# Four key blocks of an attention unit accumulate in one PSUM pair; one addition and the queries' sum go to accumulating DMAs

## The chip, the cores and the metric

One core of one Trainium2 chip runs the whole program. The metric is the device time of one execution in microseconds (us). Each kernel is given by the median of several executions and by one more execution that the hardware profiler recorded. The engines are named as in the profile: PE is TensorE's matmul side and PEld its weight loads, DVE is VectorE, ACT is ScalarE, POOL is GpSimd, and SP is SyncE, which here only issues DMAs. Every engine works through its own instructions in order and waits on semaphores of the others.

## The reference

Three stages follow one another; the change is in the first.

```python
# attention: q, k, v are (4, 8, 1152, 64) float32
q_pool = q.reshape(B, H, S // 2, 2, D).mean(axis=3)
scores = scale * np.matmul(q_pool, k.transpose(0, 1, 3, 2))
scores = scores - np.max(scores, axis=-1, keepdims=True)
attn = np.exp(scores)
attn = attn / (np.sum(attn, axis=-1, keepdims=True) + 1e-09)
x = np.matmul(attn, v)                 # 2304 tokens of 512 after a transpose
# then a dense layer: h = x @ w_in; g = h * np.cos(h); x = g @ w_out
# then a soft mixture of 8 experts with 4 slots each
```

## The kernel before

Attention handles two heads at a time, a *pair* p of 16; a pair has two halves of 288 pooled queries, and one half of a pair is a *unit* (32 units). Keys are cut into 9 *blocks* t of 128. For a unit the scores of one block are a [128 keys, 2 heads, 288 queries] tile in a PSUM pair (two banks); three such pairs (`BANKS = 3`) rotate, the fourth holds the output `o`.

- `operands` loads a pair: SP's DMAs bring `qr` (both members of each pooled pair of queries, 576 KB), `kr` (576 KB) and `vr`; DVE adds the two halves of `qr` into `qs` (`pooled`, L260); ACT makes bf16 copies `qb` and `kb` (L263).
- `maximum` finds a bound of the maximum for every query: 14 *rounds* a pair, each four bf16 matmuls into one PSUM pair (L305) and one DVE reduction of it (L310, tile `mp`). Two small transposes by PE (L317), reductions into `mc` (L324, L329) and ACT (L343) turn the result into the diagonal matrices `D`, which hold the negated maxima.
- `half_of` runs a unit. For each block, `products` (L409) multiplies keys by pooled queries in float32, `maxima` (L418) adds the negated maxima by four bf16 matmuls of ones with `D` into the same PSUM pair, ACT takes the exponential into a buffer `e` (L423, 8 buffers), and `av` (L431) accumulates `e` times values into `o`. The sums over keys are made beside it: DVE adds four of the blocks' `e` and POOL the other five (`ADD_BY`, L440), DVE joins the two (L443).
- `finish` takes the unit's output: ACT and DVE copy it out (L498, L502), PE sums over partitions (L511), small DMAs of SP spread the reciprocals (L526, L536, L540), POOL scales (L543) and makes low parts (L555).

The order is not the order of the text: `Plan` collects all operations with costs and due times, and fixes an order for every engine. The due times come from the spacing `P` of blocks and from the tables `ROUNDS` (when each round is due) and `DUES`. Two weight chunks of the next stage are decoded meanwhile (`FIRST`, lines from L707). From 389.6 us on, PE works on the dense layer (L780).

Of the kernel before, what the change touches and what calls it, by code (L numbers as in the profile page):

```python
# [10 lines left out]
FP32 = mybir.dt.float32  # L11
# [124 lines left out]
class Attention:  # L136
# [16 lines left out]
    FIRST_ROUNDS = (-13, -12, -11, -10, -9, -8, -7, -5, -7.2, -4.0, -2.3, -1.6, 0.9, 2.4)  # L153
    E_BUFS = 8

    BEHIND = 13.8

    DUES = {
        "load": 1.4, "free": 4.4, "v": 23.6, "pooled": 11.1, "qb": 3.0, "kb": -23.2, "top": -45.4,
        "diagonal": 50.2, "add": 31.2, "whole": -30.9, "take": -41.6, "join": -9.5, "sums": 14.9, "out": -15.9,  # L160
        "fold": -26.2, "inv": -14.5, "row": 30.0, "spread": 13.4, "scale": -2.4, "high": 65.4, "low": 18.3,
    }
    JOIN_BY, SCALE_BY, LOW_BY = "V", "G", "G"

# [64 lines left out]
    def operands(self, p, m):  # L229
# [11 lines left out]
        def tiles():  # L241
            self.qr[p] = self.two.tile([128, 2, NQ], FP32, tag="qr", name="qr")
            self.kr[p] = self.three.tile([128, S], FP32, tag="kr", name="kr")
            self.qs[p] = self.three.tile([128, NQ], FP32, tag="qs", name="qs")
# [20 lines left out]
        ring = lambda names, size: [(n, size, (n, p)) for n in names]  # L265
        new = ring(["kr", "qs"], 3) + ring(["qr", "qb", "kb"], 2)
        first = op(m, "SP", 0.0, tiles, new=new, early=early)
        self.q_after[p], self.k_after[p], self.s_after[p] = {}, {}, []
        late = 0.0
        for i, (a, n) in enumerate(q_parts):  # L270
            x = op(m + 0.5 * i, "SP", 0.6, lambda a=a, n=n: load_q(a, n), [first], uses=[("qr", p)],
                   more=4.2 if p else (2.4, 2.8, 3.3)[i], early=early)
            x = op(at_("pooled", 0.1 * i) if p else m, "V", 0.07 + n / 960, lambda a=a, n=n: pooled(a, n), [x], uses=[("qr", p), ("qs", p)], port=True)
            self.s_after[p].append(x)
            c = op(at_("qb", 0.1 * i) if p else m + 1.0 + i, "A", 0.07 + n / 1180, lambda a=a, n=n: copy(self.qb, self.qs, a, n), [x],
                   uses=[("qs", p), ("qb", p)])
            for y in range(0, NQ, QB):
                if a <= y < a + n:
                    self.q_after[p][y // QB] = [c]
        for i, (a, n) in enumerate(k_parts):  # L280
            x = op(m + (0.1, 0.2)[i], "SP" if p else "A", 0.6, lambda a=a, n=n: load_k(a, n), [first], uses=[("kr", p)],
                   more=5.6 if p else (2.5, 3.6)[i], early=early)
            self.s_after[p].append(x)
            for y in range(a, a + n, KC):
                self.k_after[p][y // KC] = [op(at_("kb", 0.1 * i) if p else m + 1.1 + i + y / 1e4, "A", 0.405, lambda y=y: copy(self.kb, self.kr, y, KC), [x],
                                               uses=[("kr", p), ("kb", p)])]
        self.v_after[p] = op(at_("v"), "SP", 0.6, load_v, [] if p else self.k_after[0][NC - 1], new=[("vr", 2, ("vr", p))],
                             more=4.2, early=early + late)


    def maximum(self, p):
# [55 lines left out]
        for c, rounds in enumerate(self.rounds):  # L347
            for n, (combos, x) in enumerate(rounds):
# [6 lines left out]
                       uses=users)  # L355
                new = [("mp", 2, ("mp", p))] if i == 0 else []
                d = op(t, "V", 0.868, lambda i=i, x=x: reduce(i, x), [r], new=new,
                       uses=[key] + ([] if new else [("mp", p)]))
                reds.append(d)
# [30 lines left out]
    def half_of(self, p, c):  # L390
# [11 lines left out]
        def products(t, st):  # L402
            st["ps"] = ps = self.bank(("s", u, t), "s")
            s = slice(N * c, N * c + N)
            for h in range(2):
                x = slice(64 * h, 64 * h + 64)
                for y in (0, 64):
                    w = self.kr[p][x, 128 * t + y:128 * t + y + 64]
                    nc.tensor.matmul(ps[y:y + 64, h, 0:N], w, self.qs[p][x, s], start=True, stop=False)  # L409
# [37 lines left out]
        for t in range(J):  # L447
# [17 lines left out]

            who = self.ADD_BY[t]
            if who == "P":
# [3 lines left out]
            if who not in where:  # L471
# [5 lines left out]
            before = sts[t0] if count == 1 else None  # L477
            x = op(s + due["add"] * P, who, (0.667, 1.37)[who == "G"],
                   lambda who=who, st=st, before=before, new=bool(new): add(who, st, before, new), [e, last], new=new,
                   uses=[ke] + ([("e", u, t0)] if new else [key]), port=True)  # L480
            where[who] = (count + 1, t, x)
# [98 lines left out]
    def run(self, ident, others=()):  # L580
        P, J = self.P, self.J
        pair = 2 * J * P
        self.q_after, self.k_after, self.s_after, self.v_after, self.D_after, self.reds = {}, {}, {}, {}, {}, {}
        plan = self.plan
        for p in range(self.NP):
# [933 lines left out]
```

## Time and profile before

| | us |
|---|---|
| median of 3 runs (869.24 to 871.09) | 870.83 |
| the profiled execution | 872.76 |
| its span, first to last instruction | 870.5 |
| PE busy in the span | 847.4 |
| DVE, ACT, POOL busy | 704.2, 527.7, 390.6 |

Attention fills the span from about 7.5 to 398 us, the dense layer follows, and the experts take the last 70 us. Matmuls overlap: a row's time in the profile runs to the modelled end of its last matmul, while the next row on PE starts earlier. What a piece of work costs PE is therefore read from the start of its row to the start of the next.

### The profile page before, as it was taken

To read this page: it belongs to the slowest core of one execution; us is meant where nothing else is said; L and a number is where in the kernel's file an instruction comes from. 1 tells how busy PE (TensorE), PEld (TensorE's weight loads), DVE (VectorE), ACT (ScalarE), POOL (GpSimd) and SP (SyncE) were. 2 spreads that over 40 slices of the span, in tenths; PEclk is the share of its full clock that TensorE was granted. 3 is DMA by queue.
4 is the path that set the end of the run, shared out by engine and by line. 5 is a ranking of instruction groups with operands and counts; after the bars stand their busy time and mean duration, and the time that the engine had idled before them with its cause. 6 is when DMAs were issued, how large, how long until landed. Compare 5 with 4: busy or idle time off the path is not lost.

```text
span 870.5 us, 24363 instructions
## 1 busy us (share of the span) xinstructions
PE 847.4 (97%) x9901; PEld 612.2 (70%) x9901; DVE 704.2 (81%) x1309; ACT 527.7 (61%) x1132; POOL 390.6 (45%) x381
## 2 busy tenths in 40 slices
PE   5999999999999999999999999999999999999996
PEld 3666566656666666667788888888888888877355
DVE  6999999899899888855989888888899889544423
ACT  3777777767777777774875555555555555454223
POOL 0566656766666666664554333344433333220100
PEclk9999999999999999999999999999999999999898
DMA  7033323333333233111121111110111110594897
GB/s 254 15 94 113 112 74 90 98 106 101 101 101 88 80 101 101 46 44 44 54 61 50 36 37 49 49 48 29 49 49 49 38 36 13 226 422 151 317 423 227
DMA packets 53969, 90.89 MB, mean 104 GB/s; under 512 B 21473, under 2 KB 33505, under 8 KB 49761
## 3 DMA queue, kind: packets, MB, share of 16 engines
q1 hardware_dynamic: 53568, 88.76, 31.3%
q8 instruction: 77, 1.26, 0.6%
q10 hardware_dynamic: 288, 0.59, 0.2%
q14 instruction: 36, 0.29, 0.1%
HBM read 78.71 MB, written 4.72 MB: 96 GB/s over the span
## 4 chain that ended last, share of the span: by engine, by line
PE 91%; DVE 4%; ACT 2%; issue 1%; POOL 1%; DMA 1%; SPq 0%; DVEq 0%; ACTq 0%
PE ops L780 21%; PE hps L780 21%; PE o L431 16%; PE s L409 15%; PE m L305 4%; PE s L418 4%; PE hq L1341 2%; PE so L1384 2%; PE sums L511 1%; DVE mp L310 1%; PE xtp L961 1%; PE fo L1413 1%; DMA qr<-in_q_dram 1%; PE lgp L975 1%; PE sps L1160 1%
## 5 line engine op out<-in xcount | busy, mean ns | idle before, releaser
L310 DVE TENSOR_REDUCE mp<-m 128x2 f32<-128x768 f32 x224 | 203.6, 952 | 29.8 <-PE m L305 29.4
L423 ACT ACTIVATE e<-s 128x576 f32<-128x576 f32 x288 | 176.3, 653 | 53.2 <-PE s L418 50.7
L780 PE MATMUL ops<-w,g 128*128 128x512 f32 x864 | 206.3, 391 | 2.0 <-POOL g L818 1.4
L780 PE MATMUL hps<-x,w 128*128 128x512 f32 (+1 forms) x960 | 204.5, 368 | 0.0
L780 PEld LDWEIGHTS hps<-x,w 128*128 128x128 f32 x960 | 168.0, 188 | 31.7 <-issue 1.5
L780 PEld LDWEIGHTS ops<-w,g 128*128 128x128 f32 x864 | 160.7, 188 | 36.9 <-POOL g L818 2.4
L409 PE MATMUL s<-qs,kr 64*64 64x288 f32 x2304 | 180.5, 403 | 3.2 <-DVE mp L310 3.1
L431 PE MATMUL o<-e,vr 64*64 64x288 f32 x2304 | 181.0, 406 | 0.0
L818 POOL TENSOR_TENSOR g<-r,g 128x512 fp32r<-128x512 f32 (+1 forms) x80 | 100.1, 1252 | 147.3 <-ACT g L815 121.3
L440 POOL TENSOR_TENSOR acc<-acc,e 128x576 f32<-128x576 f32 x96 | 136.6, 1423 | 3.2 <-ACT e L423 0.9
L805 ACT ACTIVATE r<-r 128x512 f32<-128x512 f32 (+1 forms) x160 | 94.0, 587 | 69.4 <-DVE r L798 67.7
L440 POOL TENSOR_TENSOR acc<-e 128x576 f32<-128x576 f32 x32 | 48.5, 1517 | 153.5 <-ACT e L423 153.5
L409 PEld LDWEIGHTS s<-qs,kr 64*64 64x64 f32 x2304 | 79.7, 133 | 44.0 <-DVE mp L310 7.4
L431 PEld LDWEIGHTS o<-e,vr 64*64 64x64 f32 x2304 | 82.7, 133 | 31.8 <-issue 7.1
L741 POOL TENSOR_TENSOR da<-da,w 128x256 f32<-128x256 f32 x64 | 49.3, 771 | 94.6 <-DVE db L730 42.1
L418 PE MATMUL s<-D,a_ones 64*64 64x288 bf16 x1152 | 87.2, 283 | 0.0
L305 PE MATMUL m<-kb,qb 64*64 64x384 bf16 x896 | 74.0, 331 | 9.3 <-ACT qb L263 7.5
L798 DVE SCALAR_TENSOR_TENSOR r<-ki,hps 128x512 f32<-128x512 int32 (+1 forms) x80 | 50.4, 631 | 36.1 <-ACT ki L795 34.1
L815 ACT CAST g<-r 128x512 fp32r<-128x512 f32 (+1 forms) x80 | 46.2, 578 | 40.0 <-DVE r L808 37.5
L795 ACT ACTIVATE ki<-hps 128x512 int32<-128x512 f32 (+1 forms) x80 | 44.0, 551 | 39.1 <-PE hps L780 38.0
L941 DVE TENSOR_TENSOR acc<-acc,ops 128x512 f32<-128x512 f32 x70 | 47.7, 685 | 22.4 <-PE ops L780 22.4
L343 ACT ACTIVATE D<-a_minus,mc 128x64 bf16<-128x64 f32 x142 | 37.4, 336 | 33.1 <-DVE mc L324 32.9
(148 smaller groups left out, 952.5 us busy)
## 6 DMA issues: line engine op xcount, KB each, us to landing
raw<-in_w_io_dram SPq DMA_DIRECT2D x64, 256.0 KB
w1t<-in_w_dram SPq DMA_DIRECT2D x15, 1024.0 KB
vr<-in_v_dram SPq DMA_DIRECT2D x16, 576.0 KB
qr<-in_q_dram SPq DMA_DIRECT2D x15, 576.0 KB
kr<-in_k_dram SPq DMA_DIRECT2D x15, 576.0 KB
w2t<-in_w2b_dram SPq DMA_DIRECT2D x8, 1024.0 KB
r<-row SPq DMA_DIRECT2D x32, 144.0 KB
late<-in_w2a_dram SPq DMA_DIRECT2D x4, 1024.0 KB
```

The source lines that it names most:

```text
L305: nc.tensor.matmul(ps[heads[c], h.start // 64, 0:self.KC], w, m, start=True, stop=True)
L310: nc.vector.tensor_reduce(out=self.mp[p][:, x], in_=st[i][:, :, 0:self.KC], axis=AX.X, op=ALU.max)
L409: nc.tensor.matmul(ps[y:y + 64, h, 0:N], w, self.qs[p][x, s], start=True, stop=False)
L418: nc.tensor.matmul(ps[y:y + 64, h, 0:N], self.ones16[x], D[x, s], start=False, stop=True)
L423: nc.scalar.activation(out=st["e"], in_=st["ps"][:, :, 0:N], func=ACTF.Exp, scale=1.0 / 16.0)
L431: nc.tensor.matmul(self.o[u][64 * h:64 * h + 64, r, 0:N], self.vr[p][x, h, t], st["e"][x, h], start=(t == 0), stop=(t == J - 1),)
L440: self.engine(who).tensor_tensor(out=acc[who], in0=x, in1=st["e"], op=ALU.add)
L741: nc.gpsimd.tensor_tensor(out=st["a"], in0=st["a"], in1=fl(half(0)), op=ALU.subtract)
L780: nc.tensor.matmul(ps, x, y, start=(i == 0 and m == 0), stop=(i == n - 1 and m == 2))
L798: nc.vector.scalar_tensor_tensor(out=st["r"], in0=st["ki"], scalar=-c, in1=x, op0=ALU.mult, op1=ALU.add)
L805: nc.scalar.activation(out=st["r"], in_=st["r"], **kw)
L818: nc.gpsimd.tensor_tensor(out=g["l"][:, i], in0=st["r"], in1=fl(g["h"][:, i]), op=ALU.subtract)
```

## The change

In every pair but the first, the blocks of a unit that stand at four places (`CHAIN`: 0, 2, 5 and 7) share one PSUM pair. POOL replaces key block b by the difference of blocks b and b + 1 for three blocks of the pair (`delta`). The first of the four gets its scores and the maxima as before; each of the other three (`link`) adds a product with a difference of keys to what stands in PSUM, so that it needs no maxima, but must wait until ACT has read the scores before it. `block(t)` permutes the blocks so that the chain's keys lie together.

The sum over `e` of one block (lower case `v` in `ADD_BY`) is made by an accumulating DMA that POOL issues, and POOL adds one block less itself, so that DVE has as many additions as before. In all pairs but the first, SP loads one half of the queries straight into `qs`, and POOL issues a DMA that accumulates the other half; DVE's addition L260 goes away there. There are 10 buffers `e` instead of 8, one `qr`, and three `mp`. The tables of due times change.

```diff
-    P = 1.28
+    P = 1.267
-    ADD_BY = "VVVGGGGVG"
+    ADD_BY = "VVvVGGGGV"
-    ROUNDS = (-10.7, -8.2, -10.4, -9.8, -3.7, -4.8, -3.3, -0.8, -8.1, 0.5, 1.6, 2.2, 7.5, 7.7)
-    E_BUFS = 8
+    ROUNDS = (-12.3, -6.4, -10.3, -16.0, -5.0, -13.7, -8.0, -1.5, -2.5, 1.0, 1.3, 5.4, 0.2, 7.5)
+    E_BUFS = 10
+    ISSUE, LANDING = 0.95, 5.5
-    BEHIND = 13.8
+    BEHIND = 10.08
...
+    CHAIN, DELTA_BY = (0, 2, 5, 7), "G"
...
         def load_q(a, n):
-            nc.sync.dma_start(out=self.qr[p][:, :, a:a + n], in_=q[:, :, a:a + n])
+            if p:
+                nc.sync.dma_start(out=self.qs[p][:, a:a + n], in_=q[:, 0, a:a + n])
+            else:
+                nc.sync.dma_start(out=self.qr[p][:, :, a:a + n], in_=q[:, :, a:a + n])
...
         def pooled(a, n):
+            if p:
+                nc.gpsimd.dma_start(out=self.qs[p][:, a:a + n], in_=q[:, 1, a:a + n], accum_op=ALU.add)
+                return
...
+        if p:
+            n = 128 * (len(self.CHAIN) - 1)
+
+            def delta():
+                x = self.kr[p]
+                self.engine(self.DELTA_BY).tensor_tensor(out=x[:, 0:n], in0=x[:, 0:n], in1=x[:, 128:128 + n], op=ALU.subtract)
...
+        def link(t, st):
+            st["ps"] = ps = sts[links[0]]["ps"]
+            s, b = slice(N * c, N * c + N), 128 * block(t)
+            for h in range(2):
+                x = slice(64 * h, 64 * h + 64)
+                for y in (0, 64):
+                    w = self.kr[p][x, b + y:b + y + 64]
+                    out = ps[y:y + 64, h, 0:N]
+                    nc.tensor.matmul(out, w, self.qs[p][x, s], start=False, stop=True, skip_group_check=True)
...
-        def add(who, st, before, new):
+        def add(who, st, before, new, by_dma=False):
...
+            if by_dma:
+                nc.gpsimd.dma_start(out=acc[who], in_=st["e"], accum_op=ALU.add)
+                return
...
+            elif t in links[1:]:
+                ks = ("s", u, links[0])
+                x = es[links[links.index(t) - 1]]
+                a = op(s, "P", 0.486, lambda t=t, st=st: link(t, st), [x, *self.delta_after[p]], uses=[ks, *uses[:2]], name="scores")
...
-FIRST_FROM, FIRST_EVERY, FIRST_DUE = 2.14, -0.96, 1000
+FIRST_FROM, FIRST_EVERY, FIRST_DUE = 2.82, -0.24, 1000
```

Three places show what this does to the order. In the rows below, a name in brackets after *waits* is the semaphore of an engine or of a DMA queue: Activation is ACT's, Pool POOL's, DMASW that of DMAs issued by POOL, DMAHW that of DMAs issued by SP or ACT. Line numbers of the changed kernel are its own: L445 products, L454 maxima, L432 links, L329 rounds, L332 their reductions, L479 additions, L477 the accumulating DMA of a block, L268 that of the queries, L306 the differences of keys.

PE in the middle of a unit, before: each block's products are followed by the maxima's weights and matmuls (four pairs of such rows a block).

```order
L418 LDWEIGHTS a_ones_130
L418 MATMUL s<-D,a_ones_130 64x288
L409 MATMUL s<-qs,kr 64x288 x4
L418 LDWEIGHTS a_ones_130
L418 MATMUL s<-D,a_ones_130 64x288
```

PE in the middle of a unit, after: a link stands between two other blocks' work, and nothing but a wait for ACT comes with it.

```order
L454 MATMUL s<-D,a_ones_130 64x288
L432 MATMUL s<-qs,kr 64x288 [waits Activation_49]
L432 MATMUL s<-qs,kr 64x288 x3
L329 LDWEIGHTS qb
L329 MATMUL m<-kb,qb 64x384 [waits Activation_49]
```

Moved: 90 links of 288 blocks have no L454 rows after them, and a round's products follow at once.

DVE from a unit's first addition to its last but one, before: the second addition follows the first at once.

```order
L440 TENSOR_TENSOR acc<-e 128x576 [waits Activation_49]
L440 TENSOR_TENSOR acc<-acc,e 128x576 [waits DVE_49,Activation_49]
L529 RECIPROCAL fold<-fold 128x36 [waits DMAHW6_49,DMAHW7_49,DMAHW1_49,DMAHW0_49]
L310 TENSOR_REDUCE mp<-m 128x2 [waits PE_49] x4
L324 TENSOR_REDUCE mc<-m 128x2x2 [waits PE_49]
L310 TENSOR_REDUCE mp<-m 128x2 [waits PE_49] x3
L440 TENSOR_TENSOR acc<-acc,e 128x576 [waits DVE_49,Activation_49]
```

The same stretch of DVE after.

```order
L479 TENSOR_TENSOR acc<-e 128x576
L332 TENSOR_REDUCE mp<-m 128x2 [waits PE_49]
L573 RECIPROCAL fold<-fold 128x36 [waits DMAHW6_49,DMAHW7_49,DMAHW1_49,DMAHW0_49]
L332 TENSOR_REDUCE mp<-m 128x2 [waits PE_49] x4
L346 TENSOR_REDUCE mc<-m 128x2x2 [waits PE_49]
L332 TENSOR_REDUCE mp<-m 128x2 [waits PE_49] x2
L479 TENSOR_TENSOR acc<-acc,e 128x576 [waits DMASW0_49,Activation_49]
```

Moved: the second addition of DVE stands seven reductions behind the first, and waits for the DMA that adds a block between them.

POOL over one unit and the head of the next, before.

```order
L440 TENSOR_TENSOR acc<-e 128x576 [waits DVE_49,Activation_49]
L543 TENSOR_TENSOR xu<-xu,r 128x288 [waits DMAHW2_49]
L440 TENSOR_TENSOR acc<-acc,e 128x576 [waits Activation_49,Pool_49]
L555 TENSOR_TENSOR x_69<-xu,x_68 128x288 [waits Activation_49]
L440 TENSOR_TENSOR acc<-acc,e 128x576 [waits Pool_49]
L741 TENSOR_TENSOR da<-da,w 128x256 [waits DVE_49]
L440 TENSOR_TENSOR acc<-acc,e 128x576 [waits Activation_49,Pool_49]
```

POOL over one unit, after.

```order
L268 DMA qs<-in_q_dram 128x576 [waits DMAHW7_49,DMASW2_49]
L477 DMA acc<-e 128x576 [waits DMASW3_49,DVE_49,Activation_49]
L479 TENSOR_TENSOR acc<-e 128x576 [waits Activation_49]
L306 TENSOR_TENSOR kr<-kr 128x384 [waits DMAHW0_49,Activation_49]
L479 TENSOR_TENSOR acc<-acc,e 128x576 [waits Activation_49,Pool_49]
L587 TENSOR_TENSOR xu<-xu,r 128x288 [waits DMAHW5_49]
L479 TENSOR_TENSOR acc<-acc,e 128x576 [waits Activation_49,Pool_49]
```

Moved: three additions of a unit instead of four, and two DMA issues and the differences ahead of and among them; the first unit of a pair shows all three, the second has the block's DMA alone.

## Rows read from the trace of the kernel before

**Rows 1.** The page, part 1: busy us, share of the span, instructions of each engine.

```profile
PE 847.4 (97%) x9901; PEld 612.2 (70%) x9901; DVE 704.2 (81%) x1309; ACT 527.7 (61%) x1132; POOL 390.6 (45%) x381
```

**Rows 2.** Time from the reductions L329, one a pair: count, ns, first and last start.

```profile
L329 DVE TENSOR_REDUCE mc<-m x16: 151/152/156, 17.1 to 368.5; 128x1 f32<-128x4 f32 x16
```

**Rows 3.** Busy us of PE, PEld, DVE, ACT, POOL (instructions), PEclk, DMA share, GB/s.

```profile
134.00:157.00 23.00, 23.00 (x452) 14.80 (x448) 21.17 (x36) 17.19 (x39) 14.99 (x15) 1.00 0.35 107
157.00:182.40 25.40, 24.02 (x464) 14.97 (x460) 23.02 (x37) 17.61 (x40) 17.53 (x16) 1.00 0.34 98
...
500.00:600.00 100.00, 100.00 (x465) 83.75 (x465) 86.86 (x193) 54.69 (x112) 39.70 (x53) 1.00 0.14 41
```

**Rows 4.** Timeline of PE in a unit: start us, us, line, operation, count.

```profile
113.20 0.66 PE L409 MATMUL s<-qs,kr 64*64 64x288 f32 x8
113.69 0.30 PE L418 MATMUL s<-D,a_ones 64*64 64x288 bf16 x4
113.81 0.67 PE L409 MATMUL s<-qs,kr 64*64 64x288 f32 x8
...
118.71 0.67 PE L431 MATMUL o<-e,vr 64*64 64x288 f32 x8
119.19 0.34 PE L305 MATMUL m<-kb,qb 64*64 64x384 bf16 x4
119.36 0.67 PE L431 MATMUL o<-e,vr 64*64 64x288 f32 x8
```

**Rows 5.** Timeline around a wait of PE: PE, then ACT, DVE and POOL.

```profile
107.07 0.72 PE L409 MATMUL s<-qs,kr 64*64 64x288 f32 x8 [1.38 <-DVE mp L310]
107.60 0.30 PE L418 MATMUL s<-D,a_ones 64*64 64x288 bf16 x4
...
107.95 0.65 ACT L423 ACTIVATE e<-s 128x576 f32<-128x576 f32 x1 [1.50 <-PE s L418]
...
104.17 1.97 DVE L440 TENSOR_TENSOR acc<-acc,e 128x576 f32<-128x576 f32 x1
106.07 1.81 DVE L310 TENSOR_REDUCE mp<-m 128x2 f32<-128x768 f32 x2
...
104.01 1.52 POOL L440 TENSOR_TENSOR acc<-e 128x576 f32<-128x576 f32 x1 [2.38 <-ACT e L423]
```

**Rows 6.** Timeline of DVE: four reductions in a row.

```profile
118.94 3.55 DVE L310 TENSOR_REDUCE mp<-m 128x2 f32<-128x768 f32 x4 [0.64 <-PE m L305]
```

**Rows 7.** Groups of 100 to 350 us: count, busy us, mean ns, idle before.

```profile
L440 POOL TENSOR_TENSOR acc<-acc,e 128x576 f32<-128x576 f32 x64 | 90.3, 1411 | 1.8 <-ACT e L423 0.5
...
L440 DVE TENSOR_TENSOR acc<-acc,e 128x576 f32<-128x576 f32 x43 | 36.3, 845 | 0.5
...
L543 POOL TENSOR_TENSOR xu<-xu,r 128x288 f32<-128x288 f32 x21 | 16.7, 797 | 0.0
...
L443 DVE TENSOR_TENSOR acc<-acc 128x576 f32<-128x576 f32 x21 | 15.8, 752 | 0.2
...
L260 DVE TENSOR_TENSOR qs<-qr 128x576 f32<-128x576 f32 x11 | 8.2, 748 | 0.0
```

**Rows 8.** A spread of 144 KB: SP's issue, its reader on POOL; queue q1 (page).

```profile
391.35 0.57 SPq L540 DMA_DIRECT2D r<-row  x1
...
393.80 0.81 POOL L543 TENSOR_TENSOR xu<-xu,r 128x288 f32<-128x288 f32 x1 [0.67 <-DMA r<-row]
...
q1 hardware_dynamic: 53568, 88.76, 31.3%
```

**Rows 9.** The start: timelines of SP, DVE and PE.

```profile
0.74 0.40 SPq L707 DMA_DIRECT2D raw<-in_w_io_dram  x1
1.20 1.98 SPq L249 DMA_DIRECT2D qr<-in_q_dram  x3
...
6.80 0.29 DVE L260 TENSOR_TENSOR qs<-qr 128x128 f32<-128x128 f32 x1 [5.07 <-DMA qr<-in_q_dram]
...
7.48 1.27 PE L305 MATMUL m<-kb,qb 64*64 64x384 bf16 x12 [7.48 <-ACT qb L263]
```

More of the change, by code (lines that the diff above doesn't have):

```diff
@@ L136 @@
 class Attention:
-    P = 1.28
+    P = 1.267
     QB, KC = 64, 384
-    ADD_BY = "VVVGGGGVG"
-    ROUNDS = (-10.7, -8.2, -10.4, -9.8, -3.7, -4.8, -3.3, -0.8, -8.1, 0.5, 1.6, 2.2, 7.5, 7.7)
-    FIRST_ROUNDS = (-13, -12, -11, -10, -9, -8, -7, -5, -7.2, -4.0, -2.3, -1.6, 0.9, 2.4)
-    E_BUFS = 8
-    BEHIND = 13.8
+    ADD_BY = "VVvVGGGGV"
+    ROUNDS = (-12.3, -6.4, -10.3, -16.0, -5.0, -13.7, -8.0, -1.5, -2.5, 1.0, 1.3, 5.4, 0.2, 7.5)
+    FIRST_ROUNDS = (-13, -12, -11, -46.4, -25.4, -23.2, -22.5, -20.0, -9.6, -8.1, -5.5, 3.8, 4.4, 11.3)
+    E_BUFS = 10
+    ISSUE, LANDING = 0.95, 5.5
+    BEHIND = 10.08
     DUES = {
-        "load": 1.4, "free": 4.4, "v": 23.6, "pooled": 11.1, "qb": 3.0, "kb": -23.2, "top": -45.4,
-        "diagonal": 50.2, "add": 31.2, "whole": -30.9, "take": -41.6, "join": -9.5, "sums": 14.9, "out": -15.9,
-        "fold": -26.2, "inv": -14.5, "row": 30.0, "spread": 13.4, "scale": -2.4, "high": 65.4, "low": 18.3,
+        "load": 3.3, "free": -6.8, "v": 20.9, "pooled": 20.4, "qb": -6.2, "kb": -23.9, "top": -52.6,
+        "diagonal": 38.5, "add": 22.6, "whole": -35.8, "take": -30.7, "join": -43.9, "sums": 12.1, "out": -8.3,
+        "fold": -36.2, "inv": 2.9, "row": 53.1, "spread": 10.4, "scale": -5.4, "high": 77.1, "low": 47.4,
+        "delta": -18.1,
     }
+    CHAIN, DELTA_BY = (0, 2, 5, 7), "G"
     JOIN_BY, SCALE_BY, LOW_BY = "V", "G", "G"
@@ L241, in tiles @@
         def tiles():
-            self.qr[p] = self.two.tile([128, 2, NQ], FP32, tag="qr", name="qr")
+            if p == 0:
+                self.qr[p] = self.one.tile([128, 2, NQ], FP32, name="qr")
             self.kr[p] = self.three.tile([128, S], FP32, tag="kr", name="kr")
+            self.mp[p] = self.three.tile([128, sum(len(x) for x in self.rounds), 2], FP32, tag="mp", name="mp")
             self.qs[p] = self.three.tile([128, NQ], FP32, tag="qs", name="qs")
@@ L265, in operands @@
         ring = lambda names, size: [(n, size, (n, p)) for n in names]
-        new = ring(["kr", "qs"], 3) + ring(["qr", "qb", "kb"], 2)
+        new = ring(["kr", "qs", "mp"], 3) + ring(["qb", "kb"], 2)
         first = op(m, "SP", 0.0, tiles, new=new, early=early)
@@ L270, in operands @@
         for i, (a, n) in enumerate(q_parts):
-            x = op(m + 0.5 * i, "SP", 0.6, lambda a=a, n=n: load_q(a, n), [first], uses=[("qr", p)],
+            x = op(m + 0.5 * i, "SP", 0.6, lambda a=a, n=n: load_q(a, n), [first], uses=[("qs", p)],
                    more=4.2 if p else (2.4, 2.8, 3.3)[i], early=early)
-            x = op(at_("pooled", 0.1 * i) if p else m, "V", 0.07 + n / 960, lambda a=a, n=n: pooled(a, n), [x], uses=[("qr", p), ("qs", p)], port=True)
+            if p:
+                x = op(at_("pooled"), "G", self.ISSUE, lambda a=a, n=n: pooled(a, n), [x], uses=[("qs", p)], port=False, more=self.LANDING)
+            else:
+                x = op(m, "V", 0.07 + n / 960, lambda a=a, n=n: pooled(a, n), [x], uses=[("qs", p)], port=True)
             self.s_after[p].append(x)
@@ L355, in maximum @@
                        uses=users)
[L356 to L358 removed]
+                d = op(t, "V", 0.868, lambda i=i, x=x: reduce(i, x), [r], uses=[key, ("mp", p)])
                 reds.append(d)
@@ L396, in half_of, with block @@
         where = {}
+        links = list(self.CHAIN) if p else []
+        others = [t for t in range(J) if t not in links]
+        def block(t):
+            return len(links) - 1 - links.index(t) if t in links else len(links) + others.index(t)
+        def link(t, st):
[7 more added lines that the diff above has]
+                    nc.tensor.matmul(out, w, self.qs[p][x, s], start=False, stop=True, skip_group_check=True)
         def scores(t, st):
@@ L403, in products @@
             st["ps"] = ps = self.bank(("s", u, t), "s")
-            s = slice(N * c, N * c + N)
+            s, b = slice(N * c, N * c + N), 128 * block(t)
             for h in range(2):
@@ L464, in half_of @@
             avs.append(b)
[L466 removed]
+            who, by_dma = self.ADD_BY[t].upper(), self.ADD_BY[t].islower()
             if who == "P":
@@ L477, in half_of @@
             before = sts[t0] if count == 1 else None
-            x = op(s + due["add"] * P, who, (0.667, 1.37)[who == "G"],
-                   lambda who=who, st=st, before=before, new=bool(new): add(who, st, before, new), [e, last], new=new,
-                   uses=[ke] + ([("e", u, t0)] if new else [key]), port=True)
+            by_dma &= not new
+            x = op(s + due["add"] * P, "G" if by_dma else who, self.ISSUE if by_dma else (0.667, 1.37)[who == "G"],
+                   lambda who=who, st=st, before=before, new=bool(new), by_dma=by_dma: add(who, st, before, new, by_dma), [e, last], new=new,
+                   uses=[ke] + ([("e", u, t0)] if new else [key]), port=not by_dma, more=self.LANDING * by_dma)
             where[who] = (count + 1, t, x)
```

11 lines of the change are left out of this document (7 added, 4 removed).

## The prediction

> **What bounds the kernel now.** I read the page's table of engines first, then the pace of attention, then what PE spends in one block, then the waits. PE is busy 97% of the span, DVE 81% [rows 1]. The reductions L329 come once a pair, sixteen of them from 17.1 to 368.5 us [rows 2]: fifteen pairs at 351.4 / 15 = 23.43 us. A quiet pair takes 23.0 us, and in it PE is busy all 23.00 us at granted clock 1.00, DVE 21.17, ACT 17.19, POOL 14.99 [rows 3]. So PE sets the pace of a quiet pair. The other 0.43 us a pair (6.4 us in all) are waits; a pair that took 25.4 us has 24.02 of PE [rows 3]. Such a wait looks like this: one addition of DVE takes 1.97 us [rows 5] where 0.75 is usual for its shape [rows 7], the reductions behind it start late, and PE, which needs their PSUM pair, stands for 1.38 us [rows 5]. POOL had begun an addition at 104.01, 0.16 us before DVE's [rows 5]. The dense layer behind attention keeps PE busy 100 of 100 us [rows 3] and is not touched, so that what attention gains at its end the kernel gains. DVE is the engine to watch: 21.2 of 23 us leave it little room.
>
> **PE: the maxima that go.** Products of one block start at 113.20, their maxima at 113.69, the next block's products at 113.81 [rows 4]. Maxima cost PE 0.12 us and products 0.49. Three of nine blocks of a unit lose them, in 15 pairs of two units: 90 x 0.12 = 10.8 us, all of it on the engine that sets the pace. A quiet pair falls from 23.0 to 23.0 - 6 x 0.12 = 22.3 us of PE. Links cost what products cost: same shape, same count.
>
> **DVE: does it follow?** It loses the queries' addition, 748 ns [rows 7], in fact 0.67 from start to start since such a row overlaps the next by some 0.08. Additions stay at three a unit and one join. 21.17 - 0.67 = 20.5 of 22.3 us is 92%, as 21.17 of 23.0 was. So DVE is no nearer to being the bound than before, and I let its waits of 6.4 us stand; they could go to nothing or double, so 6.4 either way is a bound, not a term.
>
> **ACT** does the same work: 17.2 of 22.3 us, 77%.
>
> **POOL.** It loses two additions a pair at 1.41 (two units) [rows 7] and gains the differences of 384 keys. Between 288 elements at 0.80 and 576 at 1.41 [rows 7] these are 1.0 us. So 15.0 - 2.8 + 1.0 = 13.2 us, and three DMA issues a pair on top, two of blocks and one of queries. No row shows POOL issuing a DMA. An issue by SP takes 0.57 [rows 8], and the addition that it replaces 1.41; I take 1.0, nearer to the middle than to either, since a program on POOL stands where SP has a generator. 16.2 of 22.3 us, 73%, where it was 65%: hidden. It stops being hidden where an issue takes (22.3 - 13.2) / 3 = 3.0 us. As POOL and DVE hold each other up already (DVE's `acc<-acc,e` has 845 ns on average, the join of the same shape 752 [rows 7]), two POOL additions less a pair could also give DVE up to 4 x 0.09 = 0.4 us a pair back, which I don't count.
>
> **The new wait on DVE.** The accumulating DMA of a block starts after DVE's first addition of the unit, and DVE's second addition waits for it; queued behind that addition are DVE's reductions, and for those PE waits, as in the 1.38 us above. What covers the DMA is what stands between the two additions in DVE's new order: seven reductions, a reciprocal and a small reduction in the stretch shown. Four reductions take 3.55 us [rows 6], 0.87 apart, so the cover is 7 x 0.87 + 0.4 = 6.5 us; by the same count over all units it is 5.9 to 8.7, with 7.5 in the middle, but for the last pair (2 to 2.5), where DVE has no rounds of a next pair to do. What the DMA needs: SP's spread of 144 KB is issued at 391.35, and its reader, which waited for it, starts at 393.80 [rows 8]: 2.45 us with the issue. Queue q1 moved 88.76 MB in 31.3% of 16 engines' 870.5 us [rows 8], so 326 KB a us on 16 engines; 144 KB more are 0.45 us, and reading the destination as well another 0.9. That is 2.9 to 3.8 us; an issue as long as POOL's addition makes it 4.6, and a POOL that is in the middle of another addition 6.1. Below 6.5 in each case: I take no wait.
>
> **The new waits on PE.** A link needs the exponential of the chain's block before it. From the last start of a block's matmuls: the recorded end is 0.17 later than the next row's start (113.20 + 0.66 against 113.69 [rows 4]), ACT starts 0.05 after that end (107.60 + 0.30 against 107.95) and takes 0.65 [rows 5], and PE follows within 0.05. Together 0.92 us. In the new order of PE, between a link and its predecessor stand two blocks, or a round and two of `av`, or the like; with 0.61 for a block, 0.49 for `av` or a link and 0.16 for a round [rows 4], 88 of the 90 links have 1.13 us or more, most 1.21 to 1.30. So a link has 0.2 to 0.4 us to spare, which is gone if ACT has one exponential more in front. The chain also keeps one PSUM pair for itself for most of a unit, which leaves two to rounds and other blocks. Counted in the same way, PE's work between a round and the next use of its PSUM pair stays (1.71 us in the middle, 1.74 before), between a block and the next use it falls from 1.22 to 1.13, still above 0.92. Only the transposes of the maxima get nearer to the sums behind them, 0.65 us in ten units where there were 1.13: at most a reduction (0.87) less that cover, with hops some 0.5 each, 5 us. I take 1.5 us for all of these, between nothing and 5, nearer to nothing because most places keep their cover.
>
> **The queries' and keys' loads** keep their bytes. POOL's DMA of the queries and the differences are issued more than a unit before PE needs them: no cost.
>
> **The start.** Before, SP issues a weight chunk at 0.74 (0.40 us) and the queries at 1.20, and PE starts at 7.48 because ACT and DVE waited for them [rows 9]. After, the queries come first: 0.46 us less. The first transposes of maxima also need two reductions fewer before them (1.7 us), which I keep as a bound, since PE has work that must be done anyway.
>
> **Sum.** Against the profiled execution of 872.76 us: -10.8 (maxima) - 0.5 (start) + 1.5 (new waits) = -9.8, so 863.0. The median of the runs lies 1.9 lower, 870.83; the same step from it gives 861.0.
>
> **Rivals.** *The links wait, and the gain shrinks.* 0.12 us a link cancels everything (90 x 0.12). For it: ACT is 77% busy, works in order, and copies and diagonals stand between exponentials. Against it: 0.2 to 0.4 us of room. With half of that, 0.06 a link, 861.0 + 5.4 = 866.4; with all of it, 870.8 less the start's gain and so no change.
>
> *The block's DMA comes late (slower).* DVE's second addition then holds the reductions. DVE has 22.3 - 20.5 = 1.8 us a pair of room, 0.9 a unit; each us beyond costs 30. It decides where issue and landing exceed 6.5 + 0.9 + 9.8 / 30 = 7.7 us. At 8.7 us: 1.0 x 30 us more than that, 870.8 + 30 = 901. At 8.0, 880. Against it: 2.9 to 6.1 from rows.
>
> *POOL becomes the bound (slower).* At 3.0 us an issue POOL needs the whole 22.3. As it waits for others besides, I put such a pair at 24.0 us: (24.0 - 23.43) x 15 = +8.6, 879. In the trace, DVE and POOL only lengthen each other's instructions by a tenth on average [rows 7]. The Trainium skill (SBUF — State Buffer, section on its two separate sides) says that POOL writes the descriptors of DMAs that it issues through ports which it shares with DVE, and that a DMA of 620 ns took 3100 beside a copy by DVE. By that figure POOL's pair is an estimated 13.2 + 9.3 = 22.5 us, and the time that of this rival. The same page (Who interferes with whom) says that DVE's reductions never contend; no run here shows either yet. Since 14 x 0.87 = 12.2 of DVE's 20.5 us are reductions that read PSUM, I give the rival little.
>
> *More than forecast.* With DVE's waits gone too and the start's bound: 861.0 - 6.4 - 1.7 = 853.
>
> **How the numbers follow.** Forecast, 861.0 with 856 to 866: 0.60. Links wait and part is left, 866 to 869: 0.12. No difference: 0.07. Late DMA: 0.09, POOL the bound: 0.07, together slower 0.16. More than forecast: 0.05. Within 0.2%, 1.7 us, a measurement of this kernel can't tell from no change. Faster 0.60 + 0.12 + 0.05 = 0.77, same 0.07, slower 0.16. From 855.5 to 871.0 I leave out most of slower and most of more, about 0.2.
>
> **What would show it.** Right: L329's successor at 22.3 to 22.8 us a pair, PE busy throughout a quiet pair, maxima 1152 - 360 = 792 rows of matmuls, DVE near 92%. The link rival: waits of L432 for `e`, in total over 5 us. The late DMA: DVE's L479 waiting for a DMA, and reductions late behind it. POOL: busy or issuing nearly throughout, and DVE's join or PE's sums waiting for it. The forecast is wrong if a pair takes 23.2 us or more, or if the gain of attention is lost between its end and the dense layer.

## The result: slower by 1.1%

| | before | after |
|---|---|---|
| median of seven runs each, us | 870.95 (869.24 to 872.20) | 880.55 (874.58 to 884.05) |
| ratio to before, 95% interval | | 1.011 (1.008 to 1.014) |
| profiled execution: time, span, us | 872.76, 870.5 | 874.58, 872.7 |

The forecast was 861.0 with 855.5 to 871.0. The profiled execution is the shortest of the seven; the other six have spans of 877.7 to 882.2 us.

The page of the changed kernel (its table of engines, the group of the blocks' DMA issues, the same in the list of DMAs, with KB and median us to landing) and the one-a-pair reduction:

```profile
PE 841.6 (96%) x9541; PEld 606.9 (70%) x9541; DVE 707.8 (81%) x1294; ACT 528.2 (61%) x1132; POOL 401.6 (46%) x411
...
L477 POOL DMA_DIRECT2D acc<-e x32 | 27.9, 872 | 99.0 <-ACT e L459 88.3
...
acc<-e POOLq DMA_DIRECT2D x32, 288.0 KB, 4.4
...
L351 DVE TENSOR_REDUCE mc<-m x16: 148/151/153, 14.6 to 370.8; 128x1 f32<-128x4 f32 x16
```

PE does 360 matmuls less than in [rows 1], and the first of these reductions comes 2.5 us earlier than in [rows 2], yet the last comes 2.3 us later. A pair takes 23.75 us on average instead of 23.43, and unevenly. Windows cut at starts of L351 (busy us of PE, PEld, DVE, ACT, POOL; then PE's granted clock, DMA share, GB/s):

```profile
84.10:105.40 21.30, 21.30 (x411) 13.40 (x404) 20.10 (x35) 15.85 (x37) 13.81 (x14) 1.00 0.56 135
...
105.40:135.10 29.70, 25.27 (x444) 15.79 (x440) 26.54 (x33) 18.83 (x42) 19.87 (x20) 0.91 0.45 101
...
159.00:186.70 27.70, 23.80 (x420) 14.31 (x412) 24.84 (x33) 16.89 (x39) 15.77 (x17) 0.94 0.47 110
...
257.80:280.10 22.30, 22.30 (x424) 14.22 (x420) 21.15 (x35) 16.58 (x38) 15.38 (x17) 1.00 0.54 125
```

A quiet pair runs as forecast: PE is busy without a pause for 22.3 us in the last row, with 424 matmuls where the quiet pair of [rows 3] has 452. (The pair of the first row, 21.3 us, holds fewer matmuls still.) The pairs of the second and third row are 5 to 6 us too long. In the first, the timelines of DVE, POOL and PE (start us, us, engine, line, operation; in brackets the idle time before):

```profile
123.48 0.95 DVE L332 TENSOR_REDUCE mp<-m 128x2 f32<-128x768 f32 x1
124.35 5.57 DVE L770 SCALAR_TENSOR_TENSOR da<-raw,da 128x256 int32<-128x256 int32 x1
129.83 0.95 DVE L332 TENSOR_REDUCE mp<-m 128x2 f32<-128x768 f32 x1
...
123.55 0.85 POOL L477 DMA_DIRECT2D acc<-e  x1 [1.48 <-ACT e L459]
124.11 1.12 POOL L587 TENSOR_TENSOR xu<-xu,r 128x288 f32<-128x288 f32 x1
124.88 1.30 POOL L306 TENSOR_TENSOR kr<-kr 128x384 f32<-128x384 f32 x1
125.83 1.69 POOL L479 TENSOR_TENSOR acc<-e 128x576 f32<-128x576 f32 x1
127.19 1.08 POOL L599 TENSOR_TENSOR x<-xu,x 128x288 fp32r<-128x288 f32 x1
127.94 1.68 POOL L479 TENSOR_TENSOR acc<-acc,e 128x576 f32<-128x576 f32 x1
...
125.74 0.67 PE L432 MATMUL s<-qs,kr 64*64 64x288 f32 x8
130.83 0.54 PE L329 MATMUL m<-kb,qb 64*64 64x384 bf16 x4 [4.42 <-DVE mp L332]
131.10 1.22 PE L445 MATMUL s<-qs,kr 64*64 64x288 f32 x8
```

DVE's step of the weight decode, usually 0.42 us, takes 5.57, until 0.3 us after the last of five POOL instructions that stood ready behind POOL's DMA issue. Each of these starts some 0.34 us before the recorded end of the one ahead. The reduction behind the step is late, PE waits 4.42 us for it, and then eight products take 1.22 us instead of 0.67: PE's granted clock is at its lower level, 1.2 instead of 2.4 GHz, for some us after PE has stood (0.50 in the first row below). The second long pair has the same picture, with DVE's join (L482, 5.00 us where 0.75 is usual) 0.25 us behind an issue:

```profile
131.10:135.10 4.00, 4.00 (x52) 2.67 (x48) 2.02 (x4) 1.21 (x2) 1.35 (x1) 0.50 0.05 5
...
165.16 0.88 POOL L477 DMA_DIRECT2D acc<-e  x1 [3.52 <-ACT e L459]
165.41 5.00 DVE L482 TENSOR_TENSOR acc<-acc 128x576 f32<-128x576 f32 x1
```

An issue alone does not hold DVE. In this same trace four decode steps began 0.80 us behind an issue with no POOL instruction ready behind it, and took 0.28 to 0.41 us.

### The profile page after: what moved, and what is told of

The parts are those of the page before. It is cut to its first block, busy times and chain, and to the rows that moved or that the text cites. A ratio compares the mean times of both kernels' runs of the same rounds, so it can differ in the third digit from the quotient of the medians.

```text
span 872.7 us, 23708 instructions
## 1 busy us (share of the span) xinstructions
PE 841.6 (96%) x9541; PEld 606.9 (70%) x9541; DVE 707.8 (81%) x1294; ACT 528.2 (61%) x1132; POOL 401.6 (46%) x411
## 4 chain that ended last, share of the span: by engine, by line
PE 88%; DVE 5%; DMA 2%; issue 2%; ACT 1%; SPq 1%; POOL 0%; DVEq 0%; ACTq 0%; POOLq 0%
PE hps L825 22%; PE ops L825 21%; PE o L467 14%; PE s L445 10%; PE m L329 4%; PE s L432 4%; PE s L454 2%; DVE mp L332 2%; PE hq L1386 2%; PE so L1429 2%; DMA fold<-r 2%; PE sums L555 1%; PE xtp L1006 1%; PE fo L1458 1%; PE lgp L1020 1%
## 5 line engine op out<-in xcount | busy, mean ns | idle before, releaser
L332 DVE TENSOR_REDUCE mp<-m 128x2 f32<-128x768 f32 x224 | 205.8, 947 | 24.9 <-PE m L329 23.7
L467 PE MATMUL o<-e,vr 64*64 64x288 f32 x2304 | 183.1, 410 | 0.0
L445 PE MATMUL s<-qs,kr 64*64 64x288 f32 x1584 | 129.0, 406 | 4.7 <-DVE mp L332 4.6
L467 PEld LDWEIGHTS o<-e,vr 64*64 64x64 f32 x2304 | 84.7, 135 | 28.6 <-issue 4.7
L479 POOL TENSOR_TENSOR acc<-acc,e 128x576 f32<-128x576 f32 x64 | 91.4, 1428 | 12.5 <-ACT e L459 10.8
L329 PE MATMUL m<-kb,qb 64*64 64x384 bf16 x896 | 76.6, 337 | 15.2 <-DVE mp L332 8.9
L445 PEld LDWEIGHTS s<-qs,kr 64*64 64x64 f32 x1584 | 55.6, 133 | 38.2 <-ACT e L459 10.1
L843 DVE SCALAR_TENSOR_TENSOR r<-ki,hps 128x512 f32<-128x512 int32 (+1 forms) x80 | 50.3, 629 | 32.2 <-ACT ki L840 26.2
L477 POOL DMA_DIRECT2D acc<-e x32 | 27.9, 872 | 99.0 <-ACT e L459 88.3
L329 PEld LDWEIGHTS <-qb 64*64 64x64 bf16 x896 | 32.5, 109 | 42.4 <-issue 16.1
L432 PE MATMUL s<-qs,kr 64*64 64x288 f32 x720 | 59.8, 403 | 0.3 <-ACT e L459 0.2
```

Of the source, the lines that this page charges most:

```text
L329: nc.tensor.matmul(ps[heads[c], h.start // 64, 0:self.KC], w, m, start=True, stop=True)
L432: nc.tensor.matmul(out, w, self.qs[p][x, s], start=False, stop=True, skip_group_check=True)
L467: nc.tensor.matmul(self.o[u][64 * h:64 * h + 64, r, 0:N], self.vr[p][x, h, block(t)], st["e"][x, h], start=(t == 0), stop=(t == J - 1),)
L843: nc.vector.scalar_tensor_tensor(out=st["r"], in0=st["ki"], scalar=-c, in1=x, op0=ALU.mult, op1=ALU.add)
```

## The experiments

Three theories. **A**: POOL, behind its own DMA issue, runs a ready backlog during which DVE gets no turn. **B**: the links, and a chain that keeps one PSUM pair, make PE late. **C**: the accumulating DMAs land late or crowd the loads. Later, **D**: what DVE is relieved of decides.

**The DMAs left out.** The issue in `add` is dropped, so that the sums lack a block; the rest stays in its order.

```diff
-                nc.gpsimd.dma_start(out=acc[who], in_=st["e"], accum_op=ALU.add)
```

> The changed kernel without the accumulating DMAs of the blocks (32 of 47 such DMAs; the sums over keys lack one block of nine), the order otherwise the same. A: POOL no longer stands at the DMA until DVE and ACT are done with a backlog of ready instructions behind it, and DVE's second addition waits for nothing: 860 to 869 us, 0.988 to 0.998 of before, no DVE instruction over 2.5 us. B: 874 to 886. C: as A, 860 to 869; a small DMA in its place must tell A from C.

Measured 864.98 us, ratio 0.9924 (0.9903 to 0.9944). No DVE instruction above 1.8 us in attention, granted clock 1.00. The two pairs that were long, in the same columns:

```profile
105.90:129.60 23.70, 23.61 (x449) 14.93 (x440) 21.82 (x33) 18.42 (x42) 16.49 (x17) 1.00 0.36 93
...
152.30:174.70 22.40, 22.21 (x420) 14.30 (x416) 20.59 (x34) 17.05 (x39) 14.24 (x15) 1.00 0.41 110
```

They are shorter by 29.7 - 23.7 = 6.0 and 27.7 - 22.4 = 5.3 us, together 11.3, where the two profiled spans differ by 872.7 - 861.1 = 11.6. So in the profiled executions the loss sits in the two starved pairs; what the other pairs differ by cancels. B falls. By the medians the DMAs cost 880.55 - 864.98 = 15.6 us, 4 us more than the two pairs explain. In three relatives of the changed kernel below, the profiled execution has a third starved instruction at 80 to 81 us; that this is the rest, in executions without a trace, is likely but not shown.

**The maxima back in the links.** Full products and maxima in the places of the links (on the keys as they stand, differences or not), the order and the DMAs stay.

```diff
-                    nc.tensor.matmul(out, w, self.qs[p][x, s], start=False, stop=True, skip_group_check=True)
+                    nc.tensor.matmul(out, w, self.qs[p][x, s], start=True, stop=False)
+            maxima(t, st)
```

> The changed kernel with the links replaced by full products and maxima on the same PSUM pair, in the same order and with the same waits (the differences of keys are still formed and used as keys, so that the scores are of other keys). The 360 matmuls come back, 90 x 0.12 = 10.8 us of PE. A (PE sets the pace between starvations): plus 7 to 11 us on the changed kernel, 885 to 893, 1.016 to 1.026 of before. B (PE waits at the links anyway): plus 0 to 4 us, 878 to 886. C: as A.

Measured 886.14 us, ratio 1.0178 (1.0155 to 1.0200); three DVE instructions of 5.53, 5.64 and 5.01 us. The time is in A's range and just above B's, but the step from the changed kernel, 5.6 us, lies between A's 7 to 11 and B's 0 to 4. Taking the chain away costs time and leaves the starvation: the chain is not the culprit.

**Breaks between POOL's instructions.** A memset of one column behind each of POOL's additions and products, in the changed kernel and, as a control, in the kernel before.

```diff
...
+            self.nc.gpsimd.memset(self.gaps[:, i:i + 1], 0.0)
...
```

> The changed kernel with one small memset on POOL (128 x 1, writes only) behind each of POOL's additions, subtractions and scalings of attention, the order otherwise the same. Theory A (DVE's instructions with two SBUF inputs starve while POOL runs queued instructions without a gap, as twice in the profile of the changed kernel, 5.57 and 5.00 us where 0.42 and 0.75 are usual): the memset, which reads nothing, lets DVE in; no DVE instruction of attention takes over 2.5 us, and the time is 860 to 869 us, 0.988 to 0.998 of the kernel before. Theory B (the links' waits and the two PSUM pairs left for the rest make PE late, POOL has no part in it): 874 to 886 us, 1.005 to 1.017. Theory C (the accumulating DMAs land late or crowd the loads): 874 to 886 as well.

> The kernel before with the same memsets on POOL. A: its few long DVE instructions (7.6 us over their usual times in all, at most 1.2 each) get a little shorter: 866 to 871 us, 0.995 to 1.000 of before. B and C: no difference, 870 to 872, or up to 3 us more by the memsets themselves.

Measured 884.38 us, 1.0140 (1.0084 to 1.0196), and 872.90 us, 1.0021 (1.0010 to 1.0031). Both miss A's ranges and lie in those of B and C. DVE and POOL with the memsets:

```profile
133.56 5.73 DVE L782 SCALAR_TENSOR_TENSOR da<-raw,da 128x256 int32<-128x256 int32 x1
...
133.33 1.12 POOL L597 TENSOR_TENSOR xu<-xu,r 128x288 f32<-128x288 f32 x1
134.07 0.42 POOL L230 MEMSET gaps<- 128x1 f32 x1
134.13 1.33 POOL L314 TENSOR_TENSOR kr<-kr 128x384 f32<-128x384 f32 x1
```

The memset only joins the run: the next addition starts 0.06 us behind its start. A's remedy was wrong; whether A was, needed runs that take the issue and the backlog away one at a time.

**Bytes.** The same issue, with 8 of 288 columns.

```diff
-                nc.gpsimd.dma_start(out=acc[who], in_=st["e"], accum_op=ALU.add)
+                nc.gpsimd.dma_start(out=acc[who][:, :, 0:8], in_=st["e"][:, :, 0:8], accum_op=ALU.add)
```

> The changed kernel, with the blocks' accumulating DMAs cut to 8 of their 288 columns (the other columns of that addition are left out); POOL's issue, the waits and the order stay. Theory A, sharpened by the earlier runs: what starves DVE is POOL's backlog directly behind its own DMA issue, so the bytes don't matter: one to three DVE instructions of 5.0 to 5.7 us beside such an issue remain, and 875 to 885 us. Theory C (the 288 KB crowd the loads or land late): as without these DMAs, 863 to 868 us, no DVE instruction over 2.5 us.

Measured 885.96 us, ratio 1.0178 (1.0151 to 1.0204).

```profile
81.19 5.79 DVE L775 TENSOR_SCALAR db<-da 128x256 int32<-128x256 int32 x1
...
80.39 1.20 POOL L477 DMA_DIRECT2D acc<-e  x1 [3.28 <-ACT e L459]
81.12 1.30 POOL L587 TENSOR_TENSOR xu<-xu,r 128x288 f32<-128x288 f32 x1
```

A thirty-sixth of the bytes, the same starvation: two instructions of 5.79 and 5.90 us, and two more of 3.77 and 2.84. The time is 1 us above A's range and 18 above C's: C falls. (The issue itself became longer, 1.20 instead of 0.87 us.)

**The backlog taken away.** A POOL copy of one column of `acc` behind each issue waits for the DMA's landing.

```diff
                 nc.gpsimd.dma_start(out=acc[who], in_=st["e"], accum_op=ALU.add)
...
+                nc.gpsimd.tensor_copy(out=self.gaps[:, i:i + 1], in_=acc[who][:, 0, 0:1])
```

> The changed kernel, with a POOL copy of one column behind each block's DMA that waits for its landing, so that POOL stands still for some 3.4 us and no queued instruction runs directly behind the issue; the same DMAs, bytes and additions. A: no DVE instruction over 2.5 us, no half clock in attention; 864 to 872 us, if POOL, 46 per cent busy, keeps up with 30 such waits (100 us of 355); above 880 us with waits for POOL's sums if it doesn't. C: the DMAs are all there and the time stays at 876 to 885 us. If any backlog starves DVE, with or without an issue ahead of it, the 5 us instructions remain.

Measured 945.90 us, ratio 1.0859 (1.0823 to 1.0894). What the copy waited for (us, times), and the longest of PE's waits:

```profile
  DMA acc<-e: 91.6, 28
...
PE m L331 <- ACT e L461: 22.6, 10, 3.5
```

The time pays for POOL's 91.6 us of standing, which PE's many waits reflect. But with every issue and every byte there, the longest DVE instruction of attention is 1.95 us. The join that starved at 165.41 again stands 0.24 us behind an issue, and takes its usual time:

```profile
190.30 0.88 POOL L479 DMA_DIRECT2D acc<-e  x1 [3.76 <-ACT e L461]
190.54 0.75 DVE L486 TENSOR_TENSOR acc<-acc 128x576 f32<-128x576 f32 x1
```

An issue without a backlog does not starve DVE.

**The issue taken away.** POOL adds the block itself, at the same place of the same order.

```diff
-                nc.gpsimd.dma_start(out=acc[who], in_=st["e"], accum_op=ALU.add)
+                nc.gpsimd.tensor_tensor(out=acc[who], in0=acc[who], in1=st["e"], op=ALU.add)
```

> The changed kernel, with a POOL addition of the same operands in the place of each block's DMA: the same order, chain and maxima, POOL 30 x (1.4 - 0.87) = 16 us busier. A: no issue, no starvation: no DVE instruction over 2.5 us, 863 to 870 us, below the kernel before (871). Theory B (links and two PSUM pairs make PE late): 876 us and more, as changed. C: 863 to 870 us as well.

Measured 870.94 us, ratio 0.9997 (0.9978 to 1.0015). The group of these additions, and the place that starved at 124.35 above:

```profile
L477 POOL TENSOR_TENSOR acc<-acc,e 128x576 f32<-128x576 f32 x30 | 47.8, 1594 | 80.3 <-ACT e L459 51.5 <-DVE acc L479 28.7
...
126.27 0.95 DVE L332 TENSOR_REDUCE mp<-m 128x2 f32<-128x768 f32 x1
127.14 0.77 DVE L770 SCALAR_TENSOR_TENSOR da<-raw,da 128x256 int32<-128x256 int32 x1
127.84 0.94 DVE L332 TENSOR_REDUCE mp<-m 128x2 f32<-128x768 f32 x1
...
126.14 1.50 POOL L477 TENSOR_TENSOR acc<-acc,e 128x576 f32<-128x576 f32 x1 [1.40 <-ACT e L459]
127.60 0.97 POOL L587 TENSOR_TENSOR xu<-xu,r 128x288 f32<-128x288 f32 x1
128.53 1.00 POOL L306 TENSOR_TENSOR kr<-kr 128x384 f32<-128x384 f32 x1
129.49 1.41 POOL L479 TENSOR_TENSOR acc<-e 128x576 f32<-128x576 f32 x1
```

This is the matched pair. POOL stands at the same place (80.3 us between 14 and 370 us, where it stood 94.2 before the issues) for the same reason, part of it DVE's own first addition. The same instructions pile up behind it and run back to back, and the same step of DVE falls beside them. It takes 0.77 us instead of 5.57. The only visible difference in POOL's rows is that each one now starts 0.04 to 0.05 us before the recorded end of the one ahead, not 0.34. The time misses its range by 1 us and is level with the kernel before: against leaving the block out, a POOL addition costs (870.94 - 864.98) / 32 = 0.2 us of the end.

**The issue moved back.** Each block's issue comes 3.2 us later in the written order, behind one to three POOL instructions that would pile up.

```diff
...
+        start = [t + 3.2 * (ops[i][9] == "by_dma") for i, t in enumerate(start)]
```

> The changed kernel, with each block's DMA issue moved 3.2 us later in the written order, that is behind one to three of POOL's next instructions; nothing else moves. In the changed kernel POOL stood at this issue 27 times, 83.5 us in all, until DVE had made the unit's first addition and the exponentials were there, and the instructions behind it were by then a ready backlog. Theory A (issue, then backlog, starves DVE): the waits at the issue fall below 30 us, at most one DVE instruction in attention takes over 4 us, and the time is 864 to 872 us. If the starvation has nothing to do with the backlog behind the issue: two or three such instructions as before, and 876 to 886 us.

Measured 879.45 us, ratio 1.0094 (1.0075 to 1.0112). POOL's waits at the issue (17 ns at least, in the middle and at most) and the one instruction above 4 us, with the issue ahead of it:

```profile
L477 POOLq EVENT_SEMAPHORE  x27: 17/17/17, 83.0 to 390.1; - x27
...
187.17 5.39 DVE L763 TENSOR_SCALAR da<-da 128x256 f32<-128x256 f32 x2
...
187.09 0.89 POOL L477 DMA_DIRECT2D acc<-e  x1
187.71 1.10 POOL L587 TENSOR_TENSOR xu<-xu,r 128x288 f32<-128x288 f32 x1
```

The wait at the issue is gone, as expected, but not the backlog, which I had taken for its consequence: POOL now stands one instruction earlier, and runs of four and more instructions follow 17 of the 32 issues, where it was 6 in the changed kernel. Only one of these 17 starved DVE over 4 us (the row above is of two instructions, 0.28 and 5.19 us). In 13 of the others DVE began nothing but reductions and reciprocals until the run was nearly over, which points to a second condition: what DVE begins there. In the changed kernel, too, DVE began nothing but reductions and reciprocals in the first 5 us of four of the six long runs, and none was held; the two starved instructions began 0.80 and 0.25 us behind their issue. But the two conditions do not suffice. Here a decode step began 0.49 us behind an issue, with five POOL instructions to come, and had its turn:

```profile
288.26 0.86 POOL L477 DMA_DIRECT2D acc<-e  x1
288.88 1.08 POOL L587 TENSOR_TENSOR xu<-xu,r 128x288 f32<-128x288 f32 x1
289.83 1.69 POOL L479 TENSOR_TENSOR acc<-acc,e 128x576 f32<-128x576 f32 x1
...
288.75 1.50 DVE L771 SCALAR_TENSOR_TENSOR da<-raw,da 128x256 int32<-128x256 int32 x1
```

In four more places, two in the run with memsets and two in that with 8 columns, a decode step passed so in 1.2 to 1.7 us. What tells these from the starved ones, no run shows. The time was missed, too. The pair of the starved instruction takes 32.2 us, where it takes 25.2 without the DMAs: 7.0 of the 13.9 us between the two profiled spans (875.0 and 861.1). The rest is spread over other pairs and the work behind them, and its cause stays open.

**The DMA alone, in the kernel before.** DVE's second addition of a unit becomes POOL's DMA; nothing else of the change.

```diff
+            if who == "V" and not new and p and st is sts[2]:
+                nc.gpsimd.dma_start(out=acc[who], in_=st["e"], accum_op=ALU.add)
+                return
```

> The kernel before with one thing of the change: in the 30 later units the second of DVE's additions is an accumulating DMA issued by POOL at the same place of the order; no chain, no differences, the queries' sum on DVE. It takes 30 x 0.75 = 22 us off DVE and adds 30 x 0.87 = 26 us to POOL. Theory A: POOL stands at the issue for DVE's first addition, its four additions pile up behind, and some DVE instructions take 4 us and more: 868 to 885 us. Rival D (what DVE is relieved of counts, since it was 92 per cent busy): 855 to 864 us, no DVE instruction over 2.5 us.

Measured 873.22 us, ratio 1.0015 (1.0002 to 1.0027): inside A's range, but without A's long instructions. One of 17 issues with four or more POOL instructions behind it, and DVE beside it:

```profile
80.87 0.88 POOL L441 DMA_DIRECT2D acc<-e  x1 [2.71 <-DVE da L723]
81.48 1.72 POOL L443 TENSOR_TENSOR acc<-e 128x576 f32<-128x576 f32 x1
82.86 1.09 POOL L546 TENSOR_TENSOR xu<-xu,r 128x288 f32<-128x288 f32 x1
...
80.97 1.82 DVE L310 TENSOR_REDUCE mp<-m 128x2 f32<-128x768 f32 x2 [0.45 <-PE m L305]
82.71 0.37 DVE L532 RECIPROCAL fold<-fold 128x36 f32<-128x36 f32 x1
84.08 1.82 DVE L310 TENSOR_REDUCE mp<-m 128x2 f32<-128x768 f32 x2 [1.01 <-PE m L305]
```

The same overlap of POOL's rows, and DVE passes unhindered, since in this order only reductions of PSUM and small reciprocals stand there (but for the last 0.6 us of three of the runs). Both conditions are needed; here only one is met. D falls with it: DVE was busy 19 us less (685.0 for 704.2) and the time did not fall, which fits a kernel that DVE does not bind; that the DMAs cost what DVE's relief gave is not ruled out.

**The chain without block DMAs, planned anew.** The adders of the kernel before (`VVVGGGGVG`), in two orders.

```diff
-    ADD_BY = "VVvVGGGGV"
+    ADD_BY = "VVVGGGGVG"
```

> The changed kernel with the adders of the kernel before (VVVGGGGVG, no block DMA), the order planned anew; chain, differences of keys and the queries' DMA stay. A and C: 862 to 871 us. B: 876 us and more. Against the POOL addition in the old place: within 5 us, as the two differ in the order alone.

Measured 873.71 us, ratio 1.0024 (1.0010 to 1.0038), a miss by 3 us: PE waited at attention's end for a weight chunk that this order decodes too late, `[7.36 <-ACT w L783]` ahead of its first dense product at 394.08. The second order, with `P`, `BEHIND`, five rounds, most due times and the start of the decode changed:

> The chain, the differences of keys and the queries' DMA as changed; the adders of the kernel before (VVVGGGGVG, no block DMA), and the table of due times chosen anew, so that the last weights are decoded before attention ends (in the earlier run with these adders PE waited 7.4 us for them). A: no DVE instruction over 2.5 us and 856 to 866 us, below both kernels. B (two PSUM pairs for rounds and products cost what the maxima give): 868 us and more.

Measured 866.54 us, ratio 0.9942 (0.9925 to 0.9958): faster than both kernels, 0.5 us above the range. Its one-a-pair reduction gives (360.6 - 15.3) / 15 = 23.02 us a pair; three pairs take 22.3, the forecast's quiet pair:

```profile
L346 DVE TENSOR_REDUCE mc<-m x16: 146/152/154, 15.3 to 360.6; 128x1 f32<-128x4 f32 x16
```

The same kernel with the maxima back prices the chain where nothing starves (the edit as above):

> The newly planned kernel without block DMAs (866.5 us), with full products and the 90 maxima back in the places of the links, in the same order; the differences of keys are computed but then stand for keys. It prices the chain where nothing starves. By the prediction's term, 90 x 0.12 us on a PE that does not wait: 877 us. By what the same edit cost in the changed kernel (5.6 us, there beside starvations): 872 us. If DVE and POOL set the pace and the maxima lay in PE's slack: 866 to 869 us.

Measured 875.44 us, ratio 1.0044 (1.0028 to 1.0060). The difference of the ratios is 0.0102, or 8.9 us, give or take 2 by their intervals.

## Why the prediction was wrong, step by step

- *PE sets the pace of a quiet pair, and the maxima are its price*: right. The term of 10.8 us measured 8.9, which its interval doesn't tell from 10.8; in the changed kernel, beside starvations, 5.6.
- *The start*, 0.5 us: too small. PE's first products start at 5.01 us instead of 7.48, and the first pair's last reduction 2.5 us earlier, a little more than the bound of 0.5 + 1.7.
- *Links*: right. PE waited 0.2 us for exponentials at L432, once. A round's or block's use of two remaining PSUM pairs cost little outside the starved pairs, too: with the DMAs left out, PE waited 6.2 us for DVE's reductions, 4.9 before, within the 1.5 that I took.
- *The block's DMA*: sized right. Issue 0.87 us for the 1.0 that I took, landing 4.4 us in the middle and 3.4 to 6.3 at the ends for 2.9 to 6.1. DVE waited for it once, 2.2 us. The rival of the late DMA did not come.
- *POOL is hidden*: by its busy time, yes: 13.8 and 15.4 us in the quiet pairs above for the 16.2 summed, 46% of the span. The rival "POOL the bound" gave the right sign and nearly the time, 879, for a reason that did not occur, since POOL never ran out of time.
- *DVE's waits of 6.4 us stand*: **this step failed**. I read from the mean of 845 ns beside 752 [rows 7] that DVE and POOL lengthen each other by a tenth, and let two fewer POOL additions only improve it. That mean is taken over instructions of a trace in which POOL issued no DMA in attention. The longest case, 1.97 us [rows 5], is a DVE addition beside one POOL addition. With an issue and a backlog ahead, a DVE instruction can stand through four or five POOL instructions: 5.57 and 5.00 us here, which made two pairs 6.0 and 5.3 us longer. I costed the issue as 1.0 us of POOL's time, looked at who waits *for* POOL, and did not ask what stands beside it on DVE.

I quoted the Trainium skill (SBUF — State Buffer) only for the other direction, POOL's descriptors held up by DVE. Its section "Who interferes with whom" has the rule that fits: of POOL and a DVE instruction with two SBUF inputs, or in a two-port mode, the later one blocks until the first has finished. The trace agrees on who is blocked (a decode step and the join are; reductions are not) and for a single instruction on how long: 0.77 us with POOL's addition in the issue's place. It differs behind an issue, where the blocked one waited for a whole run in eleven cases of five runs, 5.0 to 5.9 us. By the rule, one POOL instruction each, the long instructions would have been waits like that of [rows 5].

The sum by runs, from 871 (forecast: 861.0): the chain, the start and the queries' DMA, in a good order with the old adders, 866.5; in the order of the change, with POOL in place of the DMA, 870.9; with the DMA, 880.6. The DMAs gave back 15.6 us against leaving that block's addition out, and 9.6 against POOL's own. Of the gain meant, about half is there: in the good order the chain takes 8.9 us off, but with the maxima back that kernel stands 3.8 us (ratio 1.0044) above the kernel before, and no run shows of which part of the change.

Open stays why POOL's instructions overlap behind an issue, and why they then mostly, but not always, give DVE no turn; the rows show that it is so, no run shows why. A kernel with all parts of the change and an order that keeps decode steps and joins off the issues was not tried.

## To carry to other kernels

A mean over a trace says nothing of what an operation absent from it will do: before giving an engine its first DMA issues, list what stands ready behind each issue and what the engine that shares SBUF with it starts in the same microsecond. Price such an addition by the stretch it can block (here up to five instructions, 5.6 us, and PE's clock after it), times the places where both conditions meet, and not by its own 0.87 us. An addition that POOL makes itself, 1.4 us and more, was here cheaper than one that it issues.

## What the runs showed of the hardware

- Behind a DMA issue of POOL, ready POOL instructions start some 0.3 us before the recorded end of the one ahead, and a DVE instruction that uses SBUF in the blocked way (`SCALAR_TENSOR_TENSOR`, `TENSOR_TENSOR`, and `TENSOR_SCALAR` of one input too) waited 5.0 to 5.9 us, to the end of the run, in eleven cases (the changed kernel 2, memsets 3, maxima back 3, 8 columns 2, later issue 1) and 3.8 us in a twelfth; in five other places it passed in 1.2 to 1.7 us. In the runs without the blocks' issues the longest took 2.2 us. Memsets of 128x1 between them don't reliably let it in (5.1 to 5.7 us in three cases).
- An accumulating DMA of 288 KB from SBUF to SBUF takes POOL 0.87 us to issue and lands 4.4 us later; one of 8 columns of each row takes 1.20 us to issue.
- After PE had stood for 4.42 us, the profile shows its granted clock at the lower level: 0.50 from 131.1 to 135.1 us and 0.91 on average over that pair, eight products in 1.22 instead of 0.67 us. The pair with the wait of 4.4 us took 6.0 us more than without the DMAs.
